# A third bank for both score slots, and single-cell shifts on GpSimd, in a two-layer transformer kernel

## Chip, cores and metric

One core of one Trainium2 chip. The metric is device time in microseconds (us); a kernel's figure is the median of its runs.

## The reference

```python
x = A_x                                            # [1, 2048, 512] bf16
x = x + attention(layernorm(x), A_wqkv, A_wo)      # 32 heads of 16, softmax(q k^T / 4) v, then wo
x = x + ffn(layernorm(x), B_w1, B_b1, B_w2, B_b2)  # 512 -> 1792, gelu (tanh), -> 512
# and both lines once more with the same weights
```

With 2048 keys, 2048 queries, 32 heads and two layers, exp is taken of 268 million scores. That is the work this kernel is built around.

## The kernel before

The program is written out once, as five fixed instruction streams. A planner in Python keeps a clock for each engine, picks the next operation by its cost table, and the streams then run on the chip in that order, held together by semaphores alone. So an engine can't overtake its own order at run time.

A *cell* is one key tile (128 keys) by 512 query columns (of one head, or in the last part of layer 2 of two heads with 256 each): one score matmul into one PSUM bank, 4096 cells in all. ScalarE takes exp of two or three neighbouring banks in one instruction. VectorE can do a cell in place of ScalarE: it turns the scores into integers that, read as bf16, approximate the exponential, and adds three shifts; the four versions are multiplied with four scaled copies of V. These are the *D cells*. An `_Op` is (engine, cost in us, instruction, keys read and written). `acq`, `rel`, `cond` and `take` manage buffers as the order is laid out. *Fillers* are matmuls whose result nobody reads; the planner puts them into PE's gaps. *Exp's output units* (`pt`) are the buffers that exp writes and the P x V matmuls read.

```python
SLOTS = ((0, 1, 2), (3, 4))   # PSUM banks of the two score slots
PVB = 5                       # accumulator of P x V
MISC = (6, 7)                 # loose: projections, FFN, output tiles, or a D cell
SWAP = 0.5

def swap(self, op, start, cells, extra, free):      # third bank of slot 0 to VectorE
    if extra or self.lend == 2 or len(cells) < 3 or not (self.open or self.s.pools["du"]):
        return
    if self.s.clock["dve"] > start + SWAP:          # VectorE must be free soon
        return
    ...                                             # the third cell goes back, a D cell takes its bank

def scores(self):
    while True:
        sl = yield ("acq", "s")                     # a slot that everyone is done with
        ...                                         # one cell for each of its banks
        op.late = lambda op, start: (self.attach(op, start, cells, extra, free),   # D cells in loose banks
                                     self.swap(op, start, cells, extra, free))
        yield op
        self.users[sl] = 1 + any(e[1] in SLOTS[sl] for e in extra)   # ScalarE, and VectorE after a swap
        ...

def dfirst(self, pair, j, b):
    u = self.T["DU"][pair["du"]][:, 0, j, :]
    yield _Op("dve", 0.68, lambda e: e.tensor_scalar(u, self.bank(b), E_SCALE, E_BIAS, op0=ALU.mult, op1=ALU.add), ...)
    ...                                             # then the bank or the slot is released

def dchain(self, pair):                             # once both cells of a pair are there
    ...
    yield _Op("dve", 0.08 + 0.14 * n, lambda e: e.tensor_scalar(U[:, 1, 0:n, :], U[:, 0, 0:n, :], SHIFT, None, op0=ALU.add), ...)
    yield _Op("dve", 0.08 + 0.28 * n, lambda e: e.tensor_scalar(U[:, 2:4, 0:n, :], U[:, 0:2, 0:n, :], 2 * SHIFT, None, op0=ALU.add), ...)
```

A swap makes the slot depend on two readers: it is scored again when ScalarE *and* VectorE have read it (`users`).

The softmax here doesn't subtract the row's maximum and nothing guards it: scores larger than these inputs give would overflow.

## Time and profile before

| | before |
|---|---|
| time, median (range), 4 runs | 1587.8 us (1586.3 to 1589.7) |
| ScalarE, VectorE, GpSimd busy | 97%, 85%, 13% |
| exps: of two banks, of three, of one | 793, 540, 1 |
| cells of ScalarE, D cells | 3207, 889 |
| idle time of ScalarE before exps | 16.4 us |
| end of the last exp, span | 1560.8, 1587.3 us |

ScalarE is the bound; the views behind this, and what a cell and an exp cost there (0.427 us and 0.065 us), are in the prediction. The last line splits the span into attention with all that lies beside it, and the tail in which the last FFN is done.

### The profile page before, as it was taken

The numbers are of one execution on the slowest core, as the hardware profiler recorded it, in microseconds if no ns is written. First come the engines' busy times: TensorE is split into PE (matmuls) and PEld (weight loads), VectorE is DVE, ScalarE is ACT, GpSimd is POOL, SyncE is SP. The second block draws the span as 40 slices with busy tenths as digits, with TensorE's granted clock in tenths as the row PEclk, the third lists the DMA queues.
The fourth block names the chain that finished last, engine by engine and source line by source line (L and its number), as shares of the span: only waits on it lengthen the run. The fifth ranks groups of instructions, "written<-read, shape, count | busy, mean of one in ns | idle before, by whom it ended". The sixth has DMA issues, their size and how long they took to land.

```text
span 1587.3 us, 42896 instructions
## 1 busy us (share of the span) xinstructions
PE 1424.2 (90%) x18701; PEld 444.6 (28%) x18701; DVE 1352.0 (85%) x2564; ACT 1547.1 (97%) x1393; POOL 200.5 (13%) x250
## 2 busy tenths in 40 slices
PE   8998888899999898988989998888998889898988
PEld 3222222222222222222222222222222222333344
DVE  5689999888898889978788789899878988998984
ACT  7999999999999999999999999999999999999996
POOL 5200012001100201002120020122001000010000
PEclk9999999999999999999999999999999999999999
DMA  5100001241114311143111510001251105312520
GB/s 140 22 2 1 2 14 41 77 132 46 27 45 130 85 41 28 42 140 74 36 28 48 172 44 28 1 2 33 67 167 43 28 15 151 103 36 87 155 82 29
DMA packets 141767, 96.88 MB, mean 61 GB/s; under 512 B 36877, under 2 KB 141582, under 8 KB 141582
## 3 DMA queue, kind: packets, MB, share of 16 engines
q1 hardware_dynamic: 141582, 94.14, 21.2%
q8 instruction: 149, 2.44, 0.6%
q14 instruction: 36, 0.29, 0.1%
HBM read 84.41 MB, written 2.10 MB: 55 GB/s over the span
## 4 chain that ended last, share of the span: by engine, by line
ACT 67%; PE 29%; DVE 2%; POOL 1%; issue 1%; DMA 0%; ACTq 0%; POOLq 0%
ACT pt L1466 60%; PE ps L512 11%; PE ps L1137 9%; PE ps L1527 8%; ACT g L893 3%; ACT v L1466 2%; ACT kt L1466 1%; ACT q L1466 1%; DVE du L1283 1%; ACT L893 1%; ACT L1466 0%; DMA xf<-xln 0%; PE ps L1125 0%; POOL xln L602 0%; POOL rstd L588 0%
## 5 line engine op out<-in xcount | busy, mean ns | idle before, releaser
L1466 ACT ACTIVATE pt<-ps 128x1536 bf16<-128x1536 f32 (+2 forms) x1261 | 1384.2, 1246 | 15.2 <-PE ps L1137 10.3
L1137 PE MATMUL ps<-qp,kt 32*128 32x512 bf16 x4096 | 538.0, 385 | 140.8 <-ACT pt L1466 106.7
L1283 DVE TENSOR_SCALAR du<-ps 128x512 uint16<-128x512 f32 x711 | 479.7, 685 | 97.5 <-PE ps L1137 89.6
L1527 PE MATMUL ps<-pt,v 128*17 128x512 bf16 (+1 forms) x3368 | 433.8, 359 | 2.3 <-ACT pt L1466 0.8
L1527 PE MATMUL ps<-du,vc 128*17 128x512 bf16 (+1 forms) x2394 | 333.8, 358 | 2.7 <-DVE du L1346 1.4
L1137 PEld LDWEIGHTS ps<-qp,kt 32*128 32x128 bf16 x4096 | 140.6, 91 | 685.9 <-ACT pt L1466 304.2
L1346 DVE TENSOR_SCALAR du<-du 128x2048 uint16<-128x2048 uint16 x361 | 246.3, 687 | 2.5
L1085 POOL TENSOR_SCALAR qp<-q,mask 128x512 bf16<-128x512 bf16 (+1 forms) x91 | 66.3, 728 | 1013.8 <-PE ps L1137 1005.1
L512 PE MATMUL ps<-xf,wr 128*32 128x512 bf16 (+1 forms) x2400 | 170.8, 368 | 1.7 <-DMA xf<-xln 1.1
L1527 PE MATMUL ps<-du,v 128*17 128x512 bf16 (+1 forms) x798 | 154.7, 360 | 1.7 <-DVE xt L743 0.9
L1344 DVE TENSOR_SCALAR du<-du 128x1024 uint16<-128x1024 uint16 x361 | 150.5, 428 | 2.0
L1527 PEld LDWEIGHTS ps<-pt,v 128*17 128x17 bf16 x3368 | 111.8, 89 | 113.0 <-issue 72.9
L512 PE MATMUL ps<-wr,g 128*32 128x512 bf16 x1600 | 123.8, 384 | 5.5 <-ACT g L893 5.0
L1527 PEld LDWEIGHTS ps<-du,vc 128*17 128x17 bf16 x2394 | 92.5, 89 | 62.7 <-issue 27.5
L872 DVE TENSOR_SCALAR g<-ps,hb1t 128x512 bf16<-128x512 f32 (+1 forms) x112 | 79.8, 713 | 13.8 <-PE ps L512 12.9
L1527 PE MATMUL ps<-dh,vc 128*17 128x512 bf16 (+1 forms) x321 | 90.6, 358 | 0.0
L1283 DVE TENSOR_SCALAR dh<-ps 128x512 uint16<-128x512 f32 x96 | 65.8, 685 | 11.5 <-PE ps L1137 10.8
L1283 DVE TENSOR_SCALAR kt<-ps 128x512 uint16<-128x512 f32 x82 | 56.1, 684 | 20.7 <-PE ps L1137 19.9
L512 PEld LDWEIGHTS ps<-xf,wr 128*32 128x32 bf16 x2400 | 53.6, 95 | 61.5 <-issue 33.5
L602 POOL TENSOR_SCALAR xln<-x,rstd,nmr 128x512 bf16<-128x512 bf16 x58 | 58.2, 1008 | 33.3 <-DMA xf<-xln 23.2
L754 POOL TENSOR_TENSOR ott<-xt,rc 128x256 bf16<-128x256 f32 x42 | 29.5, 703 | 178.5 <-DVE rc L746 178.5
L1125 PE MATMUL ps<-vc 128*32 128x512 bf16 x476 | 50.9, 395 | 0.1
(93 smaller groups left out, 1185.2 us busy)
## 6 DMA issues: line engine op xcount, KB each, us to landing
wr<-in_B_w_dram SPq DMA_DIRECT2D x256, 256.0 KB, 2.9
wr<-in_A_wqkv_dram SPq DMA_DIRECT2D x24, 256.0 KB, 2.9
wr<-in_A_wo_dram SPq DMA_DIRECT2D x18, 256.0 KB, 2.9
out_dram<-x SPq DMA_DIRECT2D x16, 128.0 KB, 2.7
g<-in_A_wqkv_dram SPq DMA_DIRECT2D x3, 512.0 KB, 5.1
x<-in_A_x_dram SPq DMA_DIRECT2D x3, 512.0 KB, 8.0
q<-in_B_w_dram SPq DMA_DIRECT2D x3, 512.0 KB, 3.9
kt<-in_B_w_dram SPq DMA_DIRECT2D x4, 256.0 KB, 3.3
```

What stands on the lines that cost most here:

```text
L512: return [lambda e, a=a: e.matmul(out[32 * a:32 * a + 32, :], lhsT=lhsT[:, 32 * a:32 * a + 32], rhs=rhs, start=start, stop=stop, tile_posi ...
L602: yield _Op(eng, cost, lambda e: e.tensor_scalar(T["XLN"][:, x, :], T["X"][:, t, :], T["RSTD"][:, t:t + 1], T["NMR"][:, t:t + 1], op0=ALU. ...
L872: yield _Op("dve", 0.21 + n / 966, lambda e, fc=fc, pb=pb: e.tensor_scalar(T["G"][:, fc, q], pb, T["HB1T"][:, fc:fc + 1], None, op0=ALU.ad ...
L893: lambda e, g=g: e.activation(out=g, in_=g, func=ACT.Gelu_apprx_tanh), reads=gk, writes=gk, prio=2)
L1085: yield _Op("pool", 0.1 + 0.6 * w / 512, lambda e, s=s, q=q, i=i, t=t, w=w: e.tensor_scalar(T["QP"][:, s, w * i:w * i + w], q, T["MASK"][: ...
L1125: fns.append(lambda e, o=o, w=w, a=a, m=m: e.matmul(o, lhsT=w, rhs=rhs, start=start, stop=start, tile_position=(0, m * a)))
L1137: return (lambda e: e.matmul(o, lhsT=lhsT, rhs=rhs, start=True, stop=True, tile_position=(32 * a, 0)), ["K%d.%d.%d" % (l, gb, kt // 4), "Q ...
L1283: yield _Op("dve", 0.68, lambda e: e.tensor_scalar(u, self.bank(b), E_SCALE, E_BIAS, op0=ALU.mult, op1=ALU.add), reads=["B.%d" % b], write ...
L1344: yield _Op("dve", 0.08 + 0.14 * n, lambda e: e.tensor_scalar(U[:, 1, 0:n, :], U[:, 0, 0:n, :], SHIFT, None, op0=ALU.add), reads=key[0], w ...
L1346: yield _Op("dve", 0.08 + 0.28 * n, lambda e: e.tensor_scalar(U[:, 2:4, 0:n, :], U[:, 0:2, 0:n, :], 2 * SHIFT, None, op0=ALU.add), reads=k ...
L1466: yield _Op("act", 0.065 + 0.4267 * n, lambda e, src=src, dst=dst: e.activation(out=dst, in_=src, func=ACT.Exp, scale=0.25), reads=["B.%d" ...
L1527: op.fns.append(lambda e, o=o, lhsT=q[0][0][m], rhs=q[0][1][:, n * m:n * m + n], a=a, st=st, sp=sp: e.matmul(o, lhsT=lhsT, rhs=rhs, start= ...
```

## The change

Its intent: take part of the shifts off VectorE, give it in return the third bank of either slot as a source of D cells, and teach the planner that a GpSimd instruction and a VectorE shift hold each other up. The core of the diff:

```diff
-PVB = 5
-MISC = (6, 7)
+WIDE = 5
+PVB = 6
+MISC = (7, 5)          # 5 only until attention's D cells begin; then it joins the second slot
-SWAP = 0.5
+SWAP = 0.8
-EARLY = 4              # passes of layer 1 that run on the first 12 key tiles
+EARLY = 2
+SPARE = -0.5
+    def unlocked(self, op, rdy):     # the planner delays an op past the other engine's port use
+        ...
+    def widen(self):
+        yield ("acq", "wide")
+        self.slots[1].append(WIDE)
-            self.users[sl] = 1 + any(e[1] in SLOTS[sl] for e in extra)
+            self.users[sl] = 1 + any(e[1] in self.slots[sl] for e in extra)
   dfirst:
+        mine = self.s.clock["pool"] < self.s.clock["dve"] + SPARE
+        if mine:
+            pair["pool"].add(j)
   ...
-            yield from self.slot_done(0)
+            yield from self.slot_done(0 if b < 3 else 1)
+        if mine:
+            v = self.T["DU"][pair["du"]][:, 1, j, :]
+            yield _Op("pool", 0.65, lambda e: e.tensor_scalar(v, u, 1.0, float(SHIFT), op0=ALU.mult, op1=ALU.add), ...)
   dchain: the first shift on VectorE only for cells that GpSimd did not take
   norm: the transposed tile and its output buffer are taken and given back by name
```

More of the change, by code (lines that the diff above doesn't have):

```diff
@@ L202, in __init__ @@
         self.done = False
+HOLD = (0.05, 0.13)
 LATENCY = {"pe": 0.20, "act": 0.10, "dve": 0.10, "pool": 0.15, "sp": 0.1}
@@ L225, in __init__ @@
         self.filler, self.free, self.fills = None, None, set()
+        self.locks = {"pool": [], "dve": []}
+        self.fast = (0.0, 0.0)
     def pool(self, name, slots):
@@ L296, in _prio, with locking @@
         return op.prio() if callable(op.prio) else op.prio
+    def locking(self, op):
+        w = op.writes[0] if op.writes else ""
+        if op.eng == "pool":
+            return not w.startswith("RSTD")
+        return op.eng == "dve" and (w.startswith("XLN") or w.startswith("DU") and w.split(".")[2] != "0")
+    def unlocked(self, op, rdy):
+        if op.eng not in self.locks or not self.locking(op):
+            return rdy
+        now = t = max(rdy, self.clock[op.eng])
+        for a, b in self.locks["pool" if op.eng == "dve" else "dve"]:
+            if a <= t < b and not (op.eng == "dve" and a >= self.fast[0] and t < self.fast[1] + 0.02):
+                t = b
+        return t if t > now else rdy
     def landed(self, keys):
@@ L350, in run @@
                     continue
-                best.setdefault(e, []).append((th, rdy))
+                best.setdefault(e, []).append((th, self.unlocked(th.op, rdy)))
             if not best:
@@ L387, in run @@
                 self.note(start + cost - op.cost, start + cost, op)
+            if self.locking(op):
+                self.fast = (start, start + cost) if e == "dve" else self.fast
+                self.locks[e] = self.locks[e][-3:] + [(start + HOLD[0], start + cost - HOLD[1])]
             self.ops.append((e, start, cost, op.writes[0] if op.writes else ""))
@@ L737, in norm @@
         xt = T["XT"]
+        gb, ts = self.heads(seg, g)
+        yield ("acq", "xt")
         if part:
@@ L747, in norm @@
                   reads=["XT"], writes=["RC"])
-        gb, ts = self.heads(seg, g)
         o = gb % 2
+        if ts[0] == 0:
+            yield ("take", ("ott", o))
         pool = g < 6 and seg[2] == 512
@@ L757, in norm @@
                 reads=["XT", "RC"], writes=["OTT.%d.%d" % (o, t)])
+        yield ("rel", "xt", 0)
         if ts[-1] == 1:
@@ L761, in norm @@
                       writes=["OTN.%d.%d" % (gb, t % 4) for t in self.tiles(seg)])
+            yield ("rel", "ott", o)
             yield ("give", ("otn", l, seg, gb))
@@ L1030, in route @@
             return "misc"
+        if b == WIDE:
+            return "wide"
         return "misc" if q > (0 if b == MISC[0] else QUEUE if self.scored < self.rush else RUSH) or b == MISC[0] else "dbank"
@@ L1053, in setup_attention @@
         self.lead = [min(pi for pi, p in enumerate(self.pas) if p[0] == l) for l in range(NL)]
+        self.slots = [list(x) for x in SLOTS]
         self.held, self.users = [len(x) for x in SLOTS], [0] * len(SLOTS)
@@ L1072, in vcopies @@
             self.lend = 1
+            if WIDE in self.s.pools["misc"]:
+                self.s.pools["misc"].remove(WIDE)
+                self.s.pools["wide"].append(WIDE)
     def qpad(self):
@@ L1093, in free @@
         src = self.source()
-        for b in (6, 7, 0, 1, 2, 3, 4, 5) if src else ():
+        for b in (7, 5, 0, 1, 2, 3, 4) if src else ():
             k = "B.%d" % b
@@ L1178, in join @@
         if self.open is None:
-            self.open = {"du": pools["du"].pop(0), "cells": [], "full": False}
+            self.open = {"du": pools["du"].pop(0), "cells": [], "full": False, "pool": set()}
         pair = self.open
@@ L1190, in join, with swap @@
         self.nd += 1
-    def swap(self, op, start, cells, extra, free):
+    def swap(self, op, start, cells, extra, free, sl):
         if extra or self.lend == 2 or len(cells) < 3 or not (self.open or self.s.pools["du"]):
@@ L1203, in swap @@
         cells.pop()
-        f, r = self.score(c, self.s.tokens[("qp", c[0])], SLOTS[0][2])
+        f, r = self.score(c, self.s.tokens[("qp", c[0])], self.slots[sl][2])
         op.fns.pop()
@@ L1212, in swap @@
         self.alist[c[0]].insert(0, c)
-        self.join(op, d, SLOTS[0][2], extra, free)
+        self.join(op, d, self.slots[sl][2], extra, free)
     def attach(self, op, start, cells, extra, free):
@@ L1241, in scores @@
             cells = []
-            for _ in SLOTS[sl]:
+            for _ in self.slots[sl]:
                 c = self.next_act()
@@ L1248, in scores @@
                 break
-            work = list(zip(cells, SLOTS[sl]))
+            work = list(zip(cells, self.slots[sl]))
             fns, reads, writes, free, extra = [], [], [], [], []
@@ L1261, in scores @@
             op = _Op("pe", MM, fns, reads=reads, writes=writes, mode="S", slack=max(SLACK, ahead - LATE))
-            op.late = lambda op, start: (self.attach(op, start, cells, extra, free), self.swap(op, start, cells, extra, free))
+            op.late = lambda op, start, sl=sl, cells=cells, extra=extra, free=free: (self.attach(op, start, cells, extra, free), self.swap(op, start, cells, extra, free, sl))
             yield op
             self.held[sl] = len(cells)
-            self.users[sl] = 1 + any(e[1] in SLOTS[sl] for e in extra)
+            self.users[sl] = 1 + any(e[1] in self.slots[sl] for e in extra)
             for d, b, pair, j in extra:
@@ L1284, in dfirst @@
                   reads=["B.%d" % b], writes=["DU.%d.0.%d" % (pair["du"], j)] + self.over(pair["du"]))
+        mine = self.s.clock["pool"] < self.s.clock["dve"] + SPARE
+        if mine:
+            pair["pool"].add(j)
         pair["done"] = pair.get("done", 0) + 1
-        if b in MISC:
+        if b == MISC[0]:
             yield ("rel", "dbank", b)
         else:
-            yield from self.slot_done(0)
+            yield from self.slot_done(0 if b < 3 else 1)
+        if mine:
+            v = self.T["DU"][pair["du"]][:, 1, j, :]
+            yield _Op("pool", 0.65, lambda e: e.tensor_scalar(v, u, 1.0, float(SHIFT), op0=ALU.mult, op1=ALU.add),
+                      reads=["DU.%d.0.%d" % (pair["du"], j)], writes=["DU.%d.1.%d" % (pair["du"], j)])
+            pair["moved"] = pair.get("moved", 0) + 1
     def solo(self):
@@ L1343, in dchain @@
         key = [["DU.%d.%d.%d" % (du, i, j) for j in range(n)] for i in range(4)]
-        yield _Op("dve", 0.08 + 0.14 * n, lambda e: e.tensor_scalar(U[:, 1, 0:n, :], U[:, 0, 0:n, :], SHIFT, None, op0=ALU.add),
-                  reads=key[0], writes=key[1])
+        yield ("cond", lambda: pair.get("moved", 0) == len(pair["pool"]))
+        rest = [j for j in range(n) if j not in pair["pool"]]
+        if rest:
+            lo, hi = rest[0], rest[-1] + 1
+            yield _Op("dve", 0.08 + 0.14 * len(rest), lambda e: e.tensor_scalar(
+                U[:, 1, lo:hi, :], U[:, 0, lo:hi, :], SHIFT, None, op0=ALU.add),
+                reads=[key[0][j] for j in rest], writes=[key[1][j] for j in rest])
         yield _Op("dve", 0.08 + 0.28 * n, lambda e: e.tensor_scalar(U[:, 2:4, 0:n, :], U[:, 0:2, 0:n, :], 2 * SHIFT, None, op0=ALU.add),
@@ L1463, in exps @@
                 yield ("take", ("pt", r))
-            src = self.bank(SLOTS[sl][0], n).rearrange("p (j q) -> p j q", j=n)
+            src = self.bank(self.slots[sl][0], n).rearrange("p (j q) -> p j q", j=n)
             dst = self.unit(run)
@@ L1467, in exps @@
                 out=dst, in_=src, func=ACT.Exp, scale=0.25),
-                reads=["B.%d" % b for b in SLOTS[sl][:n]], writes=[k for r in run for k in self.pkeys(r)])
+                reads=["B.%d" % b for b in self.slots[sl][:n]], writes=[k for r in run for k in self.pkeys(r)])
             for r, (pi, kt, a) in zip(run, cells):
@@ L1478, in exps @@
             yield ("take", ("s", sl))
-            for b in SLOTS[sl]:
+            for b in self.slots[sl]:
                 yield ("rel", "misc", b)
@@ L1564, in run @@
         s.pool("dbank", [])
+        s.pool("xt", [0])
+        s.pool("ott", [0, 1])
+        s.pool("wide", [])
         s.route = self.route
@@ L1586, in run @@
         s.spawn(self.solo(), 4)
+        s.spawn(self.widen(), 4)
         for c in range(self.NQ):
```

## The prediction

> **What bounds the kernel now.** I read the page first: busy shares, the slices, then the chain that ended last.
>
> ```profile
> PE 1424.2 (90%) x18701; PEld 444.6 (28%) x18701; DVE 1352.0 (85%) x2564; ACT 1547.1 (97%) x1393; POOL 200.5 (13%) x250
> ...
> DVE  5689999888898889978788789899878988998984
> ACT  7999999999999999999999999999999999999996
> ...
> ACT 67%; PE 29%; DVE 2%; POOL 1%; issue 1%; DMA 0%; ACTq 0%; POOLq 0%
> ACT pt L1466 60%; PE ps L512 11%; PE ps L1137 9%; PE ps L1527 8%; ACT g L893 3%; ACT v L1466 2%; ACT kt L1466 1%; ACT q L1466 1%; DVE du L1283 1%; ACT L893 1%; ACT L1466 0%; DMA xf<-xln 0%; PE ps L1125 0%; POOL xln L602 0%; POOL rstd L588 0%
> ```
>
> ScalarE is full in every slice but the first and the last, nearly all of it the exp at L1466. VectorE is not full; GpSimd is nearly empty. So what a change is worth is told by how much exp work it takes off ScalarE. Next, the groups with shapes apart, for ScalarE and for VectorE's substitute for exp (the "D" cells: L1283 turns a score bank into an integer, L1344 and L1346 add the shifts that make its four versions):
>
> ```profile
> L1466 ACT ACTIVATE pt<-ps 128x1024 bf16<-128x1024 f32 x769 | 798.2, 1080 | 7.4 <-PE ps L1137 6.0
> L1466 ACT ACTIVATE pt<-ps 128x1536 bf16<-128x1536 f32 x491 | 740.2, 1507 | 7.8 <-PE ps L1137 4.2 <-PE ps L1527 1.3
> ```
> ```profile
> L1283 DVE TENSOR_SCALAR du<-ps 128x512 uint16<-128x512 f32 x711 | 479.7, 685 | 97.5 <-PE ps L1137 89.6
> L1346 DVE TENSOR_SCALAR du<-du 128x2048 uint16<-128x2048 uint16 x350 | 241.2, 693 | 2.5
> L1344 DVE TENSOR_SCALAR du<-du 128x1024 uint16<-128x1024 uint16 x350 | 147.9, 433 | 2.0
> L1283 DVE TENSOR_SCALAR dh<-ps 128x512 uint16<-128x512 f32 x96 | 65.8, 685 | 11.5 <-PE ps L1137 10.8
> ...
> L1344 DVE TENSOR_SCALAR dh<-dh 128x512 uint16<-128x512 uint16 x96 | 27.2, 284 | 0.4
> ```
>
> There are 4096 score matmuls (L1137), one per cell. L1283 ran 711 + 96 + 82 = 889 times (the 82 write `kt`), so ScalarE has 3207 cells, in 1334 exps: 793 in two-bank and 540 in three-bank shape (every output tile counted), one of one bank. Of the 667 visits of the three-bank slot about 127 were cut to two by a swap; the other some 760 D cells came through the two loose banks 6 and 7.
>
> What one cell costs ScalarE is not the 1507 - 1080 alone, because neighbours overlap. Between 100 and 200 us ScalarE ran 42 three-bank and 48 two-bank exps, 222 cells, with next to no idle time: at 427 ns a cell (the difference of the two means) 94.8 us, which leaves 5.2 us over 90 exps, 58 ns each. The kernel's own cost constant is 65 ns. Check on the whole: 3207 x 0.427 + 1334 x 0.065 = 1369 + 87 = 1456 us; gelu with its table loads is some 70 us, the rest the opening, the tail and 15 us of waits.
>
> For VectorE, waits and stretches:
>
> ```profile
> DVE du L1283 <- PE ps L1137: 89.6, 180, 3.1
> DVE kt L1283 <- PE ps L1137: 19.9, 22, 4.5
> ```
> ```profile
> 100.00:1500.00 1400.00, 1255.00 (x15933) 375.55 (x15925) 1225.43 (x2300) 1384.42 (x1230) 162.77 (x190) 0.99 0.22 61
> ```
>
> In the middle 1400 us (the third busy figure is VectorE) it is busy 1225 us, 87.5%, and ScalarE 98.9%. With L1283's 10.8 us for `dh`, 120 of VectorE's idle us are waits for a score bank: VectorE could take more cells if it got banks.
>
> **What the Trainium skill says.** "VectorE: DVE Perf Modes", The perf-mode tier table: 16-bit `tensor_scalar` inside SBUF runs at four elements a cycle, 693 ns for 2048. L1346 measures 693 ns for 2048, while L1283 out of PSUM takes 685 ns for only 512. So the shifts are already cheap on VectorE, and moving them off saves less than their element count suggests. "PSUM — Partial Sum Buffer", Specifications (TRN2): GpSimd cannot read PSUM, so L1283 has to stay, as it does in the change. "SBUF — State Buffer", Who interferes with whom: such a VectorE instruction in a two-port mode and a GpSimd one exclude each other, the later one waiting; an op with one PSUM source is exempt. The trace agrees:
>
> ```profile
> L602 POOL TENSOR_SCALAR xln<-x,rstd,nmr x58: 762/774/1907, 20.3 to 1513.3; 128x512 bf16<-128x512 bf16 x58
> ```
> ```profile
> L1346 DVE TENSOR_SCALAR du<-du x361: 382/683/1107, 70.2 to 1557.9; 128x2048 uint16<-128x2048 uint16 x175, 128x1024 uint16<-128x1024 uint16 x6
> ```
>
> (min/median/max.) GpSimd's 762 ns op stretches to 1907, VectorE's shift from 683 to 1107, while L1283 never exceeds 694. "GPSIMD Engine Reference", Elementwise — side-by-side cycle accounting: 769 ns for 512 elements at 1.8 cycles. The trace is a little better: GpSimd's one-input multiply of 512 bf16 has a median of 694 ns (L1085), one of 544 a median of 646 (L1068). I take 0.65 to 0.7 us for a shift there.
>
> **The change part by part.**
>
> *1. First shift on GpSimd.* A D cell now costs VectorE 889 cells' worth of L1283 601.6 + L1344 194.9 + L1346 316.7 = 1113 us, 1.252 us each: 0.677 + 0.219 + 0.356. GpSimd takes the 0.219 only when its clock is 0.5 us behind VectorE's at the cell. At a cell about every 1.3 us, with 0.1 us of latency, 0.65 us of work, some lock waits and the 200 us it already does, I guess 65% of the cells. The rest keep a shift on VectorE, then mostly of one cell (284 ns against 433 / 2), say 0.27. New cost: 0.677 + 0.356 + 0.35 x 0.27 = 1.128 us. Against it, lock collisions the other way: some 650 shifts on GpSimd hold the ports about 0.47 us each, a fifth of the time; some 750 shift ops on VectorE would meet that at a fifth and wait about 0.24 us, 36 us, if nothing steered them; the scheduler now orders around the locks, so I take 20 us.
>
> *2. Slots of three and three, swaps in both, limit 0.8 for 0.5.* Bank 5 goes from the loose banks to the second slot, and a D cell may take the third bank of either. Every score group can then offer VectorE a bank. I expect VectorE's middle share to go from 87.5% to about 92%, not higher, as a missed offer (its clock 0.85 us ahead) comes again only 0.9 to 1.3 us later.
>
> Solving for D cells at an end of 1548 us: middle 1548 - 187 = 1361 us x 0.92 = 1252, plus the 64.7 + 61.9 us of VectorE work outside 100 to 1500 us = 1379; less the 1352 - 1113 = 239 us of other work and 20 us of lock waits = 1120; over 1.128 = 993 cells, 104 more. ScalarE saves 104 x 0.427 = 44 us.
>
> *3. Number of exps.* With 3103 cells left to it, about 270 D cells through bank 7 (my estimate: projections, FFN and output tiles hold it some 60% of the time) and 723 swaps, there are (3103 + 723) / 3 = 1275 exps for 1334: 59 x 65 ns = 4 us.
>
> *4. Costs.* Three further PV matmuls per D cell, packed by four at 0.21 us: 104 x 0.16 = 17 us of PE, which has 51 + 44 = 95 us of fillers (L1125) to give up. Slots now wait for VectorE as well as for ScalarE before they are scored again, and only bank 7 serves projections and FFN once attention runs: I allow 8 us of new ScalarE idle time. EARLY 4 to 2 saves two copies and two adds (about 2.7 us of VectorE) and shortens the cover at the change of layers by 96 cells; nothing net.
>
> Sum: 1588 - 44 - 4 + 8 = 1548 us, 2.5% less.
>
> **The rivals.** (a) *Slot release becomes the wait.* A swapped cell starts up to 0.8 us late and takes 0.69, longer than a two-bank exp of 0.92 us. PE already waits for VectorE ahead of score loads (89.6 us in 152 waits for L1283). If 40 us of this reach ScalarE, the time stays near 1580. Against it: ScalarE's own waits for scores are only 10 us today. (b) *Locks eat the gain.* If GpSimd's shifts stretch as L602 did (mean 1008 for 762) and hold L1346 up, a D cell stays near 1.2 us and only the filled gaps count: about 1560. (c) *VectorE fills to 95% and GpSimd takes 80%.* Cost 1.09, roughly 1060 cells, 73 us less exp: about 1515. The idle 120 us speak for it. (d) *One loose bank starves projections and FFN* so that a layer's change leaves ScalarE idle: 1590 to 1620. The tuned EARLY and the 60% estimate speak against it.
>
> **Range and chances.** The sum is 1548; (c) sets the low side near 1512, (a) and (b) the high side near 1582. The line for 2% is 1556, only 8 us above my figure, so faster 0.62, same 0.32, slower 0.06.
>
> **What would show it.** L1283 count near 990; ScalarE cells near 3100 in about 1275 exps with two-bank ones some 720; new GpSimd shifts near 650 at 0.65 to 0.8 us; L1344 much rarer and mostly single; VectorE 91 to 93% in the middle; ScalarE idle before L1466 up from 15 to about 25 us; PE fillers fewer. I am wrong if the D count rises under 50, if ScalarE's idle time grows by over 30 us, or if L1346's mean rises over 750 ns.

## The result

1597.2 us (median of 4 runs, 1595.3 to 1599.5) against 1587.8. A ratio is the mean time of one kernel's runs over that of the other's of the same rounds, so not quite the ratio of the medians. Here it is 1.0059, with a 95% interval of 1.0042 to 1.0077: 0.6% slower, and so "same" by the 2% line, where 2.5% faster was predicted.

The page of the changed kernel, parts 1 and 4:

```profile
PE 1420.4 (89%) x18952; PEld 451.5 (28%) x18952; DVE 1330.3 (83%) x2412; ACT 1521.2 (95%) x1360; POOL 669.6 (42%) x946
...
ACT 53%; PE 41%; DVE 4%; issue 1%; POOL 1%; POOLq 0%; ACTq 0%
```

ScalarE works 26 us less than before, and yet the span is longer. The chain of waits that ended last runs through PE for 41% of the span, where it was 29%. The groups with shapes apart, of ScalarE and then of VectorE and GpSimd (busy us, mean ns, idle time before and its releasers):

```profile
L1517 ACT ACTIVATE pt<-ps 128x1024 bf16<-128x1024 f32 x727 | 720.0, 1066 | 25.8 <-PE ps L1171 23.2
L1517 ACT ACTIVATE pt<-ps 128x1536 bf16<-128x1536 f32 x503 | 710.5, 1521 | 13.1 <-PE ps L1578 9.3 <-PE ps L1171 2.8
```
```profile
L1317 DVE TENSOR_SCALAR du<-ps 128x512 uint16<-128x512 f32 x767 | 517.5, 686 | 102.3 <-PE ps L1171 95.6
L1393 DVE TENSOR_SCALAR du<-du 128x2048 uint16<-128x2048 uint16 x382 | 270.4, 719 | 5.1 <-POOL du L1329 4.4
L1390 DVE TENSOR_SCALAR du<-du 128x512 uint16<-128x512 uint16 x180 | 60.7, 345 | 0.5
```
```profile
L1329 POOL TENSOR_SCALAR du<-du 128x512 uint16<-128x512 uint16 x563 | 380.9, 679 | 536.3 <-DVE du L1317 504.2
```

With the rows for `dh` and `kt` there are 959 D cells, 70 more, and 698 of their first shifts (73%) are on GpSimd. ScalarE has 3137 cells in 1301 exps (766 of two banks, 535 of three). The idle time before exps of all shapes is 42.4 us for 16.4. VectorE did not fill up. In the middle 1400 us (third busy figure):

```profile
100.00:1500.00 1400.00, 1250.51 (x16169) 379.72 (x16161) 1208.91 (x2162) 1363.37 (x1209) 608.72 (x849) 0.99 0.22 61
```

That is 86.4%, less than before's 87.5. Who ScalarE waited for, before and after (us in total, times, longest):

```profile
ACT pt L1466 <- PE ps L1137: 10.3, 25, 0.9
ACT xf L619 <- PE ps L613: 4.6, 1, 4.6
ACT pt L1466 <- PE ps L1527: 1.3, 1, 1.3
```
```profile
ACT pt L1517 <- PE ps L1171: 26.0, 75, 1.3
ACT xf L642 <- PE ps L636: 10.9, 1, 10.9
ACT pt L1517 <- PE ps L1578: 9.3, 5, 3.7
```

The first kind of wait is for scores (L1137, L1171), the second is in the tail, and the third is for P x V matmuls (L1527, L1578) to free exp's output units.

**The account of the profiled runs.** 70 cells at 0.427 us and 33 exps at 0.065 us: 32 us less exp work. Idle time before exps: 26 us more. The last exp ends at 1560.9 us in the changed kernel and at 1560.8 in the one before, so some 6 us are lost beside the recorded idle time; an exp that starts after a wait isn't overlapped with its forerunner (a two-bank exp is recorded at 1066 ns, and back to back the next one starts 0.92 us after it), and there are 56 more waits of over 150 ns, which by my estimate is 8 us. So attention gained nothing. The tail is 32.3 us for 26.5. Together 6 us; the profiled run was the fastest of its four, hence 9.4 us between the medians.

The tail is an order of work: before, VectorE's first adds after the last exp are those of the output projection (`L785`); in the changed kernel two FFN tiles of the segment ahead (`L953`) come first, and `xf` waits 10.9 us for 4.6:

```profile
1564.34 1.28 DVE L785 TENSOR_TENSOR x<-x,ps 128x512 bf16<-128x512 bf16 x2 [0.81 <-PE ps L512]
```
```profile
1567.93 0.69 DVE L953 TENSOR_TENSOR x<-x,ps 128x512 bf16<-128x512 bf16 x1 [3.36 <-PE ps L535]
1570.74 0.69 DVE L953 TENSOR_TENSOR x<-x,ps 128x512 bf16<-128x512 bf16 x1 [2.12 <-PE ps L535]
1571.60 0.69 DVE L813 TENSOR_TENSOR x<-x,ps 128x512 bf16<-128x512 bf16 x1 [0.18 <-PE ps L535]
```

What follows asks where the 26 us of waiting come from.

**One such wait, in order of time.** A stretch of the changed kernel (start, duration, engine, line; idle time and releaser in brackets):

```profile
594.45 0.39 PE L1171 MATMUL ps<-qp,kt 32*128 32x512 bf16 x3
594.57 0.69 DVE L692 CAST q<-ps 128x512 bf16<-128x512 f32 x1
...
595.17 0.68 DVE L1317 TENSOR_SCALAR du<-ps 128x512 uint16<-128x512 f32 x1
...
595.31 1.05 PE L535 MATMUL ps<-xf,wr 128*32 128x512 bf16 x16
...
596.29 0.70 PE L1171 MATMUL ps<-qp,kt 32*128 32x512 bf16 x6
...
596.73 1.45 ACT L1517 ACTIVATE pt<-ps 128x1536 bf16<-128x1536 f32 x1 [0.50 <-PE ps L1171]
```

The three scores at 594.45 include a D cell in a slot's third bank. VectorE is busy with a projection until 595.26, then reads the bank until 595.85. ScalarE had finished its two banks of this slot at 595.32, but the slot isn't free. PE, which can't wait without wasting the time, was given 16 projection matmuls, and scores the slot at 596.29. The exp starts half a microsecond late. The profile names PE as the releaser; what was late was VectorE. (The last 0.4 us before the scores, from 595.86 on, are PE's: it was still at the projections that it had been given for the gap.)

**Counting them.** The profile leaves bank numbers out. But each engine runs its instructions in the program's order, so I paired every VectorE read and every exp of the traces with the order that the program lays down, and so with bank and slot. "Late" is a third bank's read that ends after the exp of the same slot:

| kernel | D cells in third banks, loose banks | late reads | late by, sum | idle before exps |
|---|---|---|---|---|
| before | 124, 765 | 11 | 2.8 us | 16.4 us |
| changed | 751, 208 | 80 | 26.6 us | 42.4 us |

In the changed kernel a third bank is read, in the median, 0.38 us ahead of the end of its slot's exp (before: 0.33). The room was as small before; what grew is the number of banks that have no more than this.

The same pairing tells what late reads cost. In the changed kernel the 80 exps whose slot had been held by a late read waited 13.5 us, and the 90 whose third bank had been read less than 0.2 us ahead waited 5.3 us; before, 0.9 us (11 exps) and 1.3 us (22). So 16.6 of the 26 us lie at slots that VectorE read late or nearly so. Most of the rest, 8.0 us, are waits for P x V (9.3 us for 1.3), a wait that neither the prediction nor the theories below name.

### The profile page after: what moved, and what is told of

Read it like the earlier page. It is cut to its first block, busy times and chain, and to the rows that moved or that the text cites. A ratio compares the mean times of both kernels' runs of the same rounds, so it can differ in the third digit from the quotient of the medians.

```text
span 1593.2 us, 44267 instructions
## 1 busy us (share of the span) xinstructions
PE 1420.4 (89%) x18952; PEld 451.5 (28%) x18952; DVE 1330.3 (83%) x2412; ACT 1521.2 (95%) x1360; POOL 669.6 (42%) x946
## 4 chain that ended last, share of the span: by engine, by line
ACT 53%; PE 41%; DVE 4%; issue 1%; POOL 1%; POOLq 0%; ACTq 0%
ACT pt L1517 47%; PE ps L535 15%; PE ps L1578 13%; PE ps L1171 13%; ACT g L921 2%; ACT kt L1517 1%; DVE du L1317 1%; DVE du L1393 1%; PE ps L1159 1%; ACT L921 1%; ACT v L1517 1%; ACT L1517 0%; ACT q L1517 0%; DVE xt L768 0%; POOL qp L1119 0%
## 5 line engine op out<-in xcount | busy, mean ns | idle before, releaser
L1517 ACT ACTIVATE pt<-ps 128x1024 bf16<-128x1024 f32 (+1 forms) x1230 | 1365.1, 1252 | 38.9 <-PE ps L1171 26.0
L1171 PE MATMUL ps<-qp,kt 32*128 32x512 bf16 x4096 | 522.2, 388 | 140.5 <-ACT pt L1517 106.5
L1329 POOL TENSOR_SCALAR du<-du 128x512 uint16<-128x512 uint16 x563 | 380.9, 679 | 536.3 <-DVE du L1317 504.2
L1317 DVE TENSOR_SCALAR du<-ps 128x512 uint16<-128x512 f32 x767 | 517.5, 686 | 102.3 <-PE ps L1171 95.6
L1578 PE MATMUL ps<-pt,v 128*17 128x512 bf16 (+1 forms) x3323 | 414.6, 360 | 5.1 <-ACT pt L1517 2.6
L1171 PEld LDWEIGHTS ps<-qp,kt 32*128 32x128 bf16 x4096 | 137.9, 91 | 667.0 <-ACT pt L1517 235.7
L1578 PE MATMUL ps<-du,vc 128*17 128x512 bf16 (+1 forms) x2562 | 321.9, 361 | 4.0 <-DVE du L1393 2.9
L1393 DVE TENSOR_SCALAR du<-du 128x2048 uint16<-128x2048 uint16 x385 | 271.8, 717 | 5.1 <-POOL du L1329 4.4
L1578 PE MATMUL ps<-du,v 128*17 128x512 bf16 (+1 forms) x854 | 145.5, 362 | 4.1 <-DVE xt L768 1.9
L1578 PEld LDWEIGHTS ps<-pt,v 128*17 128x17 bf16 x3323 | 106.0, 88 | 123.1 <-issue 79.1
L1578 PEld LDWEIGHTS ps<-du,vc 128*17 128x17 bf16 x2562 | 92.4, 90 | 64.4 <-issue 26.8
L1329 POOL TENSOR_SCALAR dh<-dh 128x512 uint16<-128x512 uint16 x80 | 56.5, 707 | 106.8 <-DVE dh L1317 104.3
L1578 PE MATMUL ps<-dh,vc 128*17 128x512 bf16 (+1 forms) x336 | 94.5, 361 | 0.2 <-DVE dh L1393 0.2
L1317 DVE TENSOR_SCALAR dh<-ps 128x512 uint16<-128x512 f32 x101 | 69.3, 686 | 21.4 <-PE ps L1171 20.6
L1317 DVE TENSOR_SCALAR kt<-ps 128x512 uint16<-128x512 f32 x91 | 62.4, 686 | 13.0 <-PE ps L1171 12.0
L1329 POOL TENSOR_SCALAR kt<-kt 128x512 uint16<-128x512 uint16 x55 | 38.0, 691 | 67.7 <-DVE kt L1317 65.6
L1390 DVE TENSOR_SCALAR du<-du 128x512 uint16<-128x512 uint16 (+1 forms) x192 | 65.6, 350 | 0.7
```

Source lines behind the costliest of these rows:

```text
L1171: return (lambda e: e.matmul(o, lhsT=lhsT, rhs=rhs, start=True, stop=True, tile_position=(32 * a, 0)), ["K%d.%d.%d" % (l, gb, kt // 4), "Q ...
L1329: yield _Op("pool", 0.65, lambda e: e.tensor_scalar(v, u, 1.0, float(SHIFT), op0=ALU.mult, op1=ALU.add), reads=["DU.%d.0.%d" % (pair["du"] ...
L1390: yield _Op("dve", 0.08 + 0.14 * len(rest), lambda e: e.tensor_scalar(U[:, 1, lo:hi, :], U[:, 0, lo:hi, :], SHIFT, None, op0=ALU.add), rea ...
L1517: yield _Op("act", 0.065 + 0.4267 * n, lambda e, src=src, dst=dst: e.activation(out=dst, in_=src, func=ACT.Exp, scale=0.25), reads=["B.%d" ...
L1578: op.fns.append(lambda e, o=o, lhsT=q[0][0][m], rhs=q[0][1][:, n * m:n * m + n], a=a, st=st, sp=sp: e.matmul(o, lhsT=lhsT, rhs=rhs, start= ...
```

## The experiments

Theory A: the D cells moved from loose banks, which nobody waits for, into the slots, which ScalarE lives on, so each late VectorE read now delays a slot. Rivals: B, GpSimd's shifts and the port locks; C, PE and the single loose bank; D, too few D buffers; E, PE's halved clock. All kernels gave correct results. Edits are against the changed kernel unless said; the planner's own clock served to choose candidates only. "Waits" is ScalarE's idle time before exps after the first 60 us; times are the medians beside before's of the same rounds. The changed kernel was not run again in those rounds, so it is compared with the others by the ratio to before.

| run | time, us | before | ratio | D cells | exps | waits | late reads | halved clock |
|---|---|---|---|---|---|---|---|---|
| changed | 1597.2 | 1587.8 | 1.0059 | 959 | 1301 | 42.4 | 80 | 11 |
| e1_old_banks | 1595.0 | 1590.6 | 1.0032 | 912 | 1344 | 22.5 | 20 | 4 |
| e2_no_pool | 1604.6 | 1590.6 | 1.0090 | 931 | 1299 | 41.1 | 63 | 8 |
| e3_swap_05 | 1589.0 | 1590.6 | 0.9990 | 918 | 1282 | 27.2 | 34 | 6 |
| e4_swap_03 | 1606.7 | 1590.6 | 1.0103 | 829 | 1261 | 13.2 | 23 | 6 |
| e5_float | 1586.0 | 1590.1 | 0.9970 | 939 | 1331 | 33.7 | 70 | 6 |
| e6_float_tuned | 1578.9 | 1590.1 | 0.9926 | 954 | 1346 | 28.2 | 77 | 10 |
| e7_all_pool_s05 | 1585.5 | 1590.1 | 0.9959 | 943 | 1280 | 32.5 | 54 | 11 |
| e8_du10 | 1597.1 | 1590.1 | 1.0038 | 977 | 1301 | 53.9 | 82 | 7 |
| e9_warm | 1583.0 | 1589.2 | 0.9961 | 957 | 1297 | 31.8 | 88 | 4 |
| e10_no_lock | 1582.2 | 1589.2 | 0.9958 | 971 | 1301 | 41.0 | 91 | 8 |
| e11_early4 | 1592.3 | 1589.2 | 1.0023 | 957 | 1300 | 41.5 | 87 | 9 |
| e12_float_best | 1565.8 | 1589.2 | 0.9851 | 952 | 1346 | 17.5 | 66 | 8 |
| e13_before_warm | 1589.8 | 1588.9 | 1.0001 | 889 | 1334 | 16.7 | 11 | 4 |
| e14_float_warm | 1588.2 | 1588.9 | 0.9992 | 945 | 1332 | 35.6 | 78 | 4 |
| e15_float_all | 1564.8 | 1588.9 | 0.9846 | 957 | 1318 | 18.2 | 95 | 2 |

The last column counts stretches between 60 and 1580 us in which the trace records a granted PE clock of a half, whatever their length: most last 3.4 us, a few 7 to 17. In all they are 44 us in the changed kernel and 17 us in the one before.

### One part alone: e1 and e2

```diff
 e1_old_banks: bank 5 stays loose, slots of three and two, swaps in the first slot only
-                self.s.pools["misc"].remove(WIDE); self.s.pools["wide"].append(WIDE)
-        s.spawn(self.widen(), 4)
-        if b == MISC[0]:
+        if b in MISC:
 e2_no_pool: every first shift on VectorE
-        mine = self.s.clock["pool"] < self.s.clock["dve"] + SPARE
+        mine = False
```

> The changed kernel with the bank layout of before (slots of three and two, two loose banks, swaps in the first slot only); GpSimd's shifts, the locks in the planner and the constants stay. Theory A (slots that wait for VectorE cost ScalarE more idle time than the extra D cells save): ScalarE's wait before the exps for score matmuls falls from 26 to 10-14 us, D cells fall from 959 to about 910, the time lands level with the changed kernel or better, 1585 to 1597. Rival B (GpSimd's shifts and the port locks are what costs): ScalarE's waits stay above 20 us and the time stays at 1595 or more, because the shifts are still there.

> The changed kernel with every first shift back on VectorE (one instruction for a pair, as before); the new bank layout stays. Theory A: the waits before the exps stay at 25 us or more, D cells fall to about 930 as a cell costs VectorE 1.25 us again, time 1600 to 1615, so GpSimd's share was a gain of 5 to 15 us. Rival B: the waits fall to under 15 us and the time is below 1590.

e1: ScalarE's waits for scores fall from 26.0 to 12.4 us, within A's 10 to 14 and below B's 20, with 702 shifts still on GpSimd:

```profile
ACT pt L1512 <- PE ps L1166: 12.4, 31, 2.1
```

(The 22.5 us of the table are all waits before exps.) The time came back only to 1.0032, as D cells came back too. It also shows what GpSimd's help is worth without banks to use it: VectorE's middle share is 83.5% for 87.5, and D cells rise by 23 only. e2: waits stay at 41 us without a single shift on GpSimd, so B is out as their cause. The shifts on GpSimd go with 28 more D cells and 0.3% of the time, which is no more than one order differs from another by (see e11).

### The swap limit: e3 and e4

```diff
-SWAP = 0.8
+SWAP = 0.5        # e3_swap_05;  0.3 in e4_swap_03
```

> The changed kernel with the swap limit at 0.5 us again, one constant. Theory A: fewer swaps whose VectorE read starts late, so ScalarE's waits before the exps fall from 37 to about 22 us and D cells from 959 to about 918; the two nearly cancel, time 1586 to 1596. If the waits stay where they are, the lateness of VectorE is not their cause.

> The same with 0.3 us, the other end of the scale. Theory A: ScalarE's waits before the exps go down to the 12 us of before or less, D cells to about 830, which is 130 cells or 55 us more exp work than with 0.8, and the time rises to 1605 to 1615. So cells and waits are bought one for the other. Rival C (what ScalarE waits for is the loose bank and PE, not the slots): the waits stay above 20 us here as well.

One constant, three points: limits 0.3, 0.5 and 0.8 give 829, 918 and 959 D cells, 23, 34 and 80 late reads, and 13.2, 27.2 and 42.4 us of waits. ScalarE's waits for scores in e4:

```profile
ACT pt L1517 <- PE ps L1171: 8.1, 17, 1.3
```

With few late reads they are below before's 10.3 us although just one loose bank is left for projections, FFN and D cells; that is against C. From 0.3 to 0.5 the 89 cells are worth 38 us and cost 14 us of waits; from 0.5 to 0.8 the 41 cells are worth 17.5 us and cost 15 us of waits, besides the unoverlapped starts and a tail of 32 us for 29. Of the three, 0.5 is the best, and there the new layout is level with before. (The expectation's 37 us counts waits of over 150 ns only; by that count e3 has 23.5, for the 22 expected, and e4 11.1.)

### Taking the dependence away: e5

```diff
 scores: a group is built with two cells; the third is added late
+    def third(self, op, start, cells, free, sl):
+        ...
+        b = self.slots[sl][2]
+        if b not in self.busy and all(... read of bank b ends by start + THIRD ...):
+            op.fns.append(self.score(c, ..., b)[0])
+            op.writes.append("B.%d" % b)
+            return
+        cells.pop()                       # left out this once; the cell goes back to its list
+        ...
-            self.users[sl] = 1 + any(e[1] in self.slots[sl] for e in extra)
+            self.users[sl] = 1
 dfirst:
-            yield from self.slot_done(0 if b < 3 else 1)
+            self.busy.discard(b)
```

> The changed kernel with one thing taken away: a slot's next score group no longer waits for VectorE. If VectorE has not read the slot's third bank by then, the group is issued with two cells and the third bank is left out once. Banks, GpSimd's shifts, swap limit and buffers stay. Theory A (late reads of third banks make ScalarE wait): ScalarE's waits before the exps fall from 42 us to 26-32, releases of a slot by a late VectorE read go to none, D cells stay near 940, exps rise to about 1330, time 1582 to 1592. Rival C (PE and the single loose bank make ScalarE wait): the waits stay at 38 us or more and the time at 1595 or more.

VectorE still reads 70 third banks late, but no slot waits for it: the next group goes out with two cells. ScalarE's waits in e5 (`L1173` are the scores, `L1600` the P x V matmuls):

```profile
ACT pt L1538 <- PE ps L1600: 18.9, 7, 8.8
ACT pt L1538 <- PE ps L1173: 8.5, 17, 2.2
```

Its waits for scores fall from 26.0 us in 75 to 8.5 in 17, under those of before. The exps whose third bank was read late, or less than 0.2 us ahead, wait 0.8 and 0.9 us here, for 13.5 and 5.3. This is the shown part of theory A: nothing but the dependence was removed (and what the order makes of it). Yet the sum is 33.7 us, over the 26 to 32 expected, because another wait grew: for P x V to free exp's output units, 18.9 us for 9.3, of which 8.8 us is one stall near 1500 us that lies inside a 17 us stretch of halved clock. The time fell by 0.9 points, within the expected range.

### More buffers, and more shifts on GpSimd: e8 and e7

```diff
 e8_du10:            -DU = 9        +DU = 10       -PT_RING = 19   +PT_RING = 15
 e7_all_pool_s05:    -SWAP = 0.8    +SWAP = 0.5    -SPARE = -0.5   +SPARE = 0.0
```

> The changed kernel with one more buffer for a D cell in flight (ten for nine, paid with four exp units, 15 for 19). In the program's own order 279 of the changed kernel's score groups passed over a D cell because no buffer was free, against 89 before. Rival D (missing buffers hold the D count, and with them the time): D cells rise to about 977 and the time falls by 5 us or more, to under 1592. Theory A: the D cells rise all the same, but the extra swaps make more slots late, waits before the exps go over 50 us, and the time is the same or worse, 1596 to 1608.

> The changed kernel, slots still waiting for VectorE, with the swap limit at 0.5 and all first shifts offered to GpSimd. Theory A: D cells near 940 and waits near 28 us, time 1577 to 1588. Rival B: more shifts on GpSimd give longer shifts on VectorE (over 750 ns a pair) and the time is 1590 or more.

e8: buffers did hold the D count (977 for 959), so D is right on that; but the time did not move, 1597.1, and the waits rose to 53.9 us. Four exp units were the price, and the waits for P x V doubled (9.3 to 19.4 us), so the rise can't be put on late reads alone (82 for 80). e7: 934 shifts on GpSimd bring the pair shift on VectorE to 740 ns, just under B's limit, and the time into A's range. The waits, 32.5 us, are over A's 28. More shifts on GpSimd did no harm here: against e3, from which e7 differs in `SPARE` alone, the ratio fell from 0.9990 to 0.9959.

### The clock, the lock model, EARLY: e9, e10, e11

```diff
 e9_warm:     -WARM = 0.38   +WARM = 0.5          # fillers until PE's recent share is 0.5
 e10_no_lock: unlocked() returns rdy unchanged
 e11_early4:  -EARLY = 2     +EARLY = 4
```

> The changed kernel with fillers allowed up to a share of 0.5 of PE's recent time for 0.38, so that PE's clock drops less often. In the profile of the changed kernel the clock was halved 11 times between 60 and 1580 us, in that of before 4 times. Rival E (the halved clock delays the score matmuls and is what ScalarE waits for): drops fall to 5 or fewer, ScalarE's waits before the exps to 30 us or less, time under 1588. Theory A: the waits stay at 35 us or more and the time at 1590 or more, whatever the clock does.

> The changed kernel ordered as if GpSimd and VectorE never kept each other waiting; the instructions are the same kinds. If the lock model of the change is of use, the pair shift on VectorE goes from 716 ns to over 750, the waits before the exps rise over 45 us and the time is 1597 or more. If it only ties the planner's hands, the D cells rise to about 971 and the time falls to 1585 to 1592.

> The changed kernel with EARLY at 4 again. If the shorter cover at the change of layers was costly, the time falls by 5 us or more; I expect no difference beyond 4 us either way, D cells about 957, the stretch after the last exp 29 us for 32.

e9 came in between the theories: drops to 4, time under E's limit, waits of 31.8 us just over it. Split by place, the picture is clear. Exp waits from 2 us before to 10 us after a halved-clock stretch, and all others:

| | before | changed | e4_swap_03 | e9_warm |
|---|---|---|---|---|
| near a halving | 4.6 us | 13.8 us | 3.5 us | 3.5 us |
| elsewhere | 11.8 us | 28.5 us | 9.7 us | 28.3 us |

So of the 26 us, 17 are elsewhere, untouched by e9 and gone with the swaps in e4; most are waits for scores (20.8 us for 6.4). 9 lie near halvings, and 5.5 of these 9 are two waits for P x V. Whether the halved clock *makes* those 9 isn't shown, since e9's order changed with its fillers.

The run lists say more on rival E than the traces do. They give the mean granted clock of every execution, and within each kernel, one fixed program run 4 to 6 times, the executions with the lower clock took longer: over these 16 kernels, the changed one and e1 to e15, the correlation is -0.73 to -1.00, and the slope is 0.8 us for 0.001 of clock in the median (0.5 to 1.7). A halved stretch of 3.4 us takes 0.001 off the mean of a span. The changed kernel ran at 0.984 in the mean, the one before at 0.992 to 0.993 in the rounds of the experiments. An estimate from these figures: some 7 of the 9.4 us between the two go with the clock, and so do some 9 of the 14 us by which e9 (0.995) is faster than the changed kernel, and some 4 of e5's 11 (0.989). A correlation doesn't tell which of the two makes the other, and the 7 us are not on top of the waits but another cut through the same time. So E is not refuted; it is the rival that stays.

e10: the lock model is no gain. Without it the pair shift takes 740 ns for 719 (both without `kt`), short of the 750 that I had set, D cells rise to 971, and the time is 1582.2 us, below the 1585 to 1592 expected. That is no proof that the planner's caution cost 15 us: the clock was 0.994 for 0.984, which by the slope above goes with 8 us, 12 D cells are 5 us, and orders differ by as much for no known reason (below). Its profiled run was the slowest of six (1589), so its 41 us of waits are on the high side. e11: 1592.3 us for 1597.2, with a tail of 29 us; D cells and waits hardly move. That is more than the 4 us that I had allowed either way, but one order differs from another by 5 us and more (e6 and e12, below, by 13), so I claim nothing from it.

### Do the causes add up, and does it carry: e6, e12, e13, e14, e15

```diff
 e6_float_tuned:  e5 with SPARE = 0.0,   SWAP = 0.65, EARLY = 3, THIRD = 0.05 (e5: 0.2)
 e12_float_best:  e5 with SPARE = -0.25, SWAP = 0.65, EARLY = 3, THIRD = 0.05
 e13_before_warm: the kernel before with WARM = 0.5
 e14_float_warm:  e5 with WARM = 0.5
 e15_float_all:   e5 with WARM = 0.5, no lock model, SPARE = 0.0, SWAP = 0.6, EARLY = 3
```

> The same decoupling with every first shift on GpSimd that the locks let through (limit 0.0), swap limit 0.65 and EARLY 3, the best of my candidates. Theory A: D cells near 954 with waits before the exps near 25 us, time 1570 to 1582, faster than both kernels by about 1%. If GpSimd's port locks are a cost of their own (rival B), some 950 to 1000 shifts there push the pair shift on VectorE over 750 ns and the time stays above 1588.

> The decoupled slots of e5_float with the shift limit at -0.25, swap limit 0.65 and EARLY 3. Theory A: D cells about 952, ScalarE's waits before the exps near 22 us, time 1567 to 1577, at least 0.8% faster than before. If it lands at e6_float_tuned's 1579 or above, the planner's small differences between such versions mean nothing on the chip.

> The kernel before with the filler limit at 0.5, the control of e9_warm: in the program's order only fillers are added. Before had 4 halvings of the clock and 4.6 us of exp waits near them. If the halved clock costs what lies near it, the time falls by 2 to 5 us, to 1584 to 1588, with waits away from halvings unchanged at 12 us. If the fillers get in the way as much as they help, nothing changes.

> The changed kernel with both suspected causes taken away, decoupled slots of e5_float and fillers of e9_warm, its other constants kept. If the two causes are separate, waits near clock halvings are under 5 us and waits elsewhere 17 to 22 us, and the time is 1573 to 1583. If they are the same cause, the time is that of e9_warm or e5_float, 1583 to 1587.

> The candidate with everything that helped: decoupled slots, fillers to 0.5, no lock model, shifts on GpSimd wherever its clock allows (limit 0.0), swap limit 0.6, EARLY 3. D cells about 957, waits before the exps under 20 us, time 1560 to 1570. If some 950 shifts on GpSimd unplanned for the locks hurt, the pair shift on VectorE goes over 760 ns and the time over 1575.

e6 came out as expected in time and D cells, with waits of 28.2 us for 25 and a pair shift of 751 ns, so B's sign came without B's loss of time.

e13 settles less than I hoped: the fillers did not remove before's 4 halvings, so its unchanged time says only that extra fillers cost nothing there. e14 missed its range. Halvings fell to 4 and waits near them to 3.2 us, and the waits for scores stayed low, but waits for P x V were 20.4 us, one of them 10.7 us. (That one begins as a halved stretch ends, at 1493 us, and is counted elsewhere only because its exp starts more than 10 us later; so the split by place doesn't separate the two causes here.)

```profile
ACT pt L1538 <- PE ps L1600: 20.4, 8, 10.7
ACT pt L1538 <- PE ps L1173: 8.9, 19, 2.2
```

So with the changed kernel's constants, once the slots no longer wait, exp's output units run short, and that is a limit of its own. What makes P x V late there I did not separate.

In e12 and e15 both kinds of wait are small (e12's below), and they are by far the fastest versions, 1.5% under before: 1565.8 and 1564.8 us for 1589. (e5, e6, e7, e9 and e10 are under before by 0.3 to 0.7%, with intervals that leave out 1. By the 2% line every run here is the same as before.) In e15 the pair shift is at 757 ns under 945 shifts on GpSimd. What e12 and e15 owe to each constant was not separated; e6 and e12 differ in one constant of the order and by 13 us.

```profile
ACT pt L1538 <- PE ps L1173: 6.4, 17, 2.1
...
ACT pt L1538 <- PE ps L1600: 4.9, 3, 2.3
```

## Why the prediction was wrong

**Right: what a D cell costs VectorE (step 1).** Predicted 1.128 us. Measured: L1317 649.2, L1390 84.7, L1393 350.2, together 1084.1 us over 959 cells, 1.130. GpSimd took 73% of the shifts for the guessed 65%, at 679 ns; the pair shift rose to 716 ns (`kt` included), under the 750 that would have refuted it. Part of the agreement is luck. The prediction set 20 us of lock waits apart from its 1.128; the measured 1.130 holds them, by my estimate 27 us (a single shift of a D cell takes 345 to 350 ns in the mean for 284 before, the pair shift 719 for 693), and GpSimd's larger share made up for it.

**Wrong in size: the middle share of VectorE at 92% (step 2).** It fell to 86.4%, and the D count rose by 70, not 104. VectorE did get its 0.12 us a cell back but had no cells to spend it on: it waited for score banks as before (95.6 us in the `du` row, for 89.6). In the program's order each score group now carried at most one D cell, where before 39 carried two. Of the 360 groups without one, 279 had no free buffer. (The 89 that e8's expectation gives for before counts groups of three cells only; with those of two it is 176.) e8 shows that one more buffer brings 18 cells. I had counted banks and overlooked buffers. Worth 34 x 0.427 = 14.5 us, with 1.7 us more for 26 exps over the predicted 1275. Rival (c), with 1060 cells, could not have come true at all: 1024 is the most that the scaled V copies allow, and the low side of the range rested on it.

**The step that failed: "I allow 8 us of new ScalarE idle time" (step 4).** It was 26 us, with some 6 more of unoverlapped starts. Of the 26, 16.6 lie at slots that VectorE read late or nearly so. This mechanism was in the prediction as rival (a), slot release becomes the wait, and I set it aside because ScalarE waited only 10 us for scores before. That figure came from a kernel with 124 swapped banks; the change made them 751. The late reads should have been counted and carried over with the number of swaps: they grew from 11 to 80, somewhat faster than the swaps. e4 and e5 show it from two sides, few swaps and no dependence. The other 8 us are waits for P x V, which no rival held.

**Not foreseen: the tail,** 6 us, and the lower clock, both above. None of the prediction's three signs of being wrong came (70 D cells, 26 us of idle time, 716 ns), and yet it missed by 49 us: no limit was set for the sum of several smaller misses.

The misses add up: 14.5 + 1.7 + 18 (waits) + 6 (starts) + 6 (tail) = 46 of the 49 us between 1548 and 1597; the rest is what the profiled runs and the medians differ by. Rival (b), the locks, and (d), starving projections, were rightly held small: e2 and e7 for the first, e4 for the second.

**Open:** whether the lower clock makes the changed kernel's time longer or comes with it; why P x V is late in the changed kernel, e5, e8 and e14; what settles the order in the tail (26 to 32 us over all versions).

## What to carry to other kernels

When a buffer gets a second reader, its release is the later of the two, so count how often the second one will be last before adding up what the sharing saves; a wait that is small with few sharers tells the cost of one share, not of many. Where the two readers can be parted, by leaving the shared piece out once when it isn't back yet, try that as well as tuning a limit: here it turned a loss of 0.6% into a gain of 0.3% with the other constants kept (tuning the limit alone brought it level), and 1.5% with several tuned. And taking work off an engine gained little here until a free bank and a free buffer let it start more work (e1, e8). Last, compare the granted clocks of two kernels before explaining a difference of half a per cent.

## What the Trainium skill lacked or had wrong

- "SBUF — State Buffer", Who interferes with whom, says that the later of a two-port VectorE instruction and a GpSimd one fully blocks. The runs agree (GpSimd's shift: 612 ns shortest, 618 median, 1167 longest), but the page gives no measure of what unplanned overlap costs on average. Here 599 to 950 shifts on GpSimd took the mean pair shift on VectorE from 692 ns to between 713 and 757, and the kernel ordered around the locks was no faster than the one that wasn't (1597.2 us, e10: 1582.2, at a higher clock).
- "GPSIMD Engine Reference", Elementwise — side-by-side cycle accounting, calls 1.8 cycles an element the best case of a tight loop and gives 769 ns for 512 elements. A one-input uint16 multiply and add of 512 elements has a median of 618 ns here (times on GpSimd are rough in this profile).
- "PSUM — Partial Sum Buffer" tells which engines may read a bank. No page speaks of a group of banks read by two engines and released by the later: 80 late reads of 751, and 13.5 us of waits at the exps behind them.
